# Turning keys and queries by DMA transposes, SBUF to SBUF, in four late steps of a retention and gated-unit kernel

## The chip, the cores and the metric

The kernel runs on one core of one Trainium2 chip. The metric is the device time of one execution in microseconds (us). Ratios and intervals are over fast runs alone; a run is called slow when it lies over 1.5% above the fastest run of the same kernel.

## The reference, cut to what matters

```python
# attention part: 8 batches, 8 heads, 576 positions, head size 64
scores = q @ k.T / 8                       # per batch and head
out    = (scores * Dmat) @ v               # Dmat[i, j] = gamma_h ** (i - j) for i >= j, else 0
x      = out, heads side by side           # 8 x 576 x 512
# gated part
gate   = sigmoid(causal 5-tap convolution of x, per channel)
result = (gate * (x @ w_val)) @ w_out      # 8 x 576 x 512
```

## The kernel before

The sequence is cut into pieces of 256 positions, and a remainder of 64. There are 20 steps, 0 to 19; steps 6, 9, 16 and 19 are the remainders of two batches at once. For each step GpSimd scales and casts keys and queries to bf16 (kb, qb). TensorE turns them in blocks of 128x128 (tpk, tpq, into PSUM), ScalarE copies the keys back and VectorE the queries (kt, qt). TensorE then makes scores (sc) from both, and the share of the carried state (o) from qt.

```python
def transp(s, which="kq"):
    ...
    for nm in which:
        tp = glp.tile([P, HP, R, P], BF16, tag="gps", name="tp" + nm)
        for hp in range(HP):
            for rr in range(R):
                nc.tensor.transpose(tp[:, hp, rr, :], src[:, rr, 2*hp:2*hp+2, :]..., ident)
        t = at.tile([P, HP, R, P], BF16, tag=f"{nm}t{R}", name=nm + "t", bufs=1 + R)
        copy(TE[nm == "q"], t, tp)          # keys: ScalarE, queries: VectorE
        r[nm + "t"] = t
```

The order of work in each step is written out by hand. `T` turns step s+1, `Sa` and `Sb` are the two halves of the scores of step s, `I` its share of the state, `X` the new state of step s+1, and numbers are spaces filled with gated work.

```python
FULL = [["Sa", "T", "4.45", "X", "XS", "0.0", "I", "Sb", "Q3", "G3", "4.9", "Vb", "Va", "E", "B"],
        ["Sa", "4.5", "X", "I", "XS", "Sb", "0.0", "Q3", "G3", "T", "7.15", "Vb", "Va", "E", "B"]]
...
for s in range(NS):
    if s + LOOK < NS:                       # LOOK = 4
        load(s + LOOK)                      # three DMAs from SyncE's queue
    if s > 1 and s + 2 < NS:
        cast(s + 2)                         # GpSimd
    for op in FULL[n] ...:
```

All loads and all output stores are issued by SyncE, one after another.

Of the kernel before, what the change touches and what calls it, by code (L numbers as in the profile page):

```python
# [15 lines left out]
BF16 = mybir.dt.bfloat16  # L16
# [15 lines left out]
def kernel(  # L32
# [10 lines left out]
    nc = tc.nc  # L43
# [3 lines left out]
    P = 128  # L47
# [4 lines left out]
    HP = H // 2  # L52
# [7 lines left out]
    TPS, DSS, CAP = False, False, 2.0  # L60
    PB, EV, TE = [4, 2, 2], "DA", "AD"
    C1, LO = "PPP", "1vo23"
    PATH, TAIL, LASTS = {9: {2: 'D', 3: 'A'}, 11: {2: 'D', 3: 'A'}, 10: {0: 'D', 1: 'A', 2: 'D', 3: 'A'}}, ['w', 'w', 't9.201234', 'w', 'p10.301234', 's10.30', 't10.001234', 's10.31', 'w', 'w', 'w', 'w', 'c9.0', 't10.201234', 'w', 'p11.301', 'w', 'p11.323', 'w', 'p11.34', 's11.30', 'w', 's11.31', 'c11.0', 'v9.0', 'v9.1', 'v9.2', 'v9.3', 't11.201234', 'o9.0', 'o9.1', 'v11.0', 'v11.1', 'v11.2', 'v11.3', 'o11.0', 'o11.1', 'v10.0', 'v10.1', 'v10.2', 'v10.3', 'z10'], [['Sa', '4.5', 'I', 'Sb', 'Q5', 'G5', 'T', '7.15', 'Vb', 'p9.301234', 'Va', 's9.30', 's9.31', 'E', 'B'], ['1.8', 'I', 'Sr', 'p10.101234', '6.65', 'Vr', 's10.10', 'E', 'B', 's10.11']]
    SPL, REMD = 0, [2, 0, 2, 0]
    VC = "P"
# [6 lines left out]
    at = ctx.enter_context(tc.tile_pool(name="at", bufs=3))  # L72
# [19 lines left out]
    NS = len(steps)  # L92
# [130 lines left out]
    def cast(s):  # L223
        u, bb, n = steps[s]
        r = st[s]
        R = 1 if bb is None else 2
        shp = [P, R, H, D]
        f0 = n * 2
        nb = 2 if bb is None else 4
        kb = cs.tile(shp, BF16, tag=f"kb{R}", name="kb", bufs=nb)  # L230
        qb = cs.tile(shp, BF16, tag=f"qb{R}", name="qb", bufs=nb)
        vb = cs.tile(shp, BF16, tag=f"vb{R}", name="vb", bufs=nb)

        how = C1 if s == 1 else "PP" + VC[s % len(VC)]
        for e, dst, src, f in ((how[0], kb, r["kf"], fk), (how[1], qb, r["qf"], fq)):
            (nc.vector if e == "D" else nc.gpsimd).tensor_tensor(  # L236
                dst, src.rearrange("p h r d -> p r h d"),
                f[:, f0:f0 + R, :].unsqueeze(3).to_broadcast(shp), op=ALU.mult)
        vsrc = r["vf"].rearrange("p h r d -> p r h d")
        if how[2] == "A":  # L240
            nc.scalar.copy(vb, vsrc)
        else:
            nc.gpsimd.tensor_copy(vb, vsrc)  # L243
        r.update(qb=qb, kb=kb, vb=vb)

    def transp(s, which="kq"):
        if s >= NS:
            return
        r = st[s]
        R = 1 if steps[s][1] is None else 2  # L250
        for nm in which:
            src = r[nm + "b"]
            tp = (scp if TPS else glp).tile([P, HP, R, P], BF16, tag="sc" if TPS else "gps", name="tp" + nm)
            for hp in range(HP):
                for rr in range(R):
                    nc.tensor.transpose(tp[:, hp, rr, :],  # L256
                                        src[:, rr, 2 * hp:2 * hp + 2, :].rearrange("p a d -> p (a d)"), ident)
            t = at.tile([P, HP, R, P], BF16, tag=f"{nm}t{R}", name=nm + "t", bufs=1 + R)
            copy(TE[nm == "q"], t, tp)
            r[nm + "t"] = t  # L260

    def copy(engine, dst, src):
        if engine == "A":
            nc.scalar.copy(dst, src)  # L264
        else:
            nc.vector.tensor_copy(dst, src)  # L266
# [454 lines left out]
    for s in range(NS):  # L721
# [4 lines left out]
        if s > 1 and s + 2 < NS:  # L726
            cast(s + 2)
        for op in (PART if bb is None else FIRST if s == 0 else SECOND if s == 1 else FULL[n]) if s < NS - len(LASTS) \
# [16 lines left out]
            elif op == "I":  # L745
                inter(s)
            elif op == "T":
                transp(s + 1)
            elif op in ("Tk", "Tq"):
                transp(s + 1, op[1])  # L750
            elif op == "C1":
                cast(1)
            elif op == "C2":
                cast(2)
            elif op[0] == "Q":
                pull(3, int(op[1]))
# [23 lines left out]
            elif op == "B":  # L780
                b = 2 * u + (bb or 0)
# [44 lines left out]
```

## Time and profile before

| | before |
|---|---|
| median, us (all runs of the first comparison) | 182.06 (181.06 to 184.66, 4 runs) |
| span of the profiled run, us | 181.1 |
| TensorE busy | 158.2 us, 87% |
| VectorE / ScalarE / GpSimd busy | 69% / 58% / 60% |
| time of the load and store queue's packets, share of 16 DMA engines | 78.6% |

A busy share is an average over the whole span. What matters here is when: the DMA engines are full for two thirds of the run (8 or 9 tenths in slices 1 to 26 of forty) and mostly free after that (0 to 5 tenths from slice 28 on), TensorE is full nearly to the end (8 or 9 tenths in slices 20 to 38). The prediction below shows those rows, the chain, and the timelines of TensorE and SyncE around step 15.

### The profile page before, as it was taken

Reading aid. Unit: us, or ns where it says so; the run is one execution under the profiler, and the core shown is the slowest. Engines: PE = TensorE matmul, PEld = TensorE weight load, DVE = VectorE, ACT = ScalarE, POOL = GpSimd, SP = SyncE. Lnnn points to the kernel's source line nnn. Section 1 sums busy time; section 2 is a strip of 40 time slices with the busy share of each in tenths; the row PEclk is TensorE's granted clock in tenths of the full one; section 3 lists DMA queues with packets and bytes.
Section 4 is the critical chain, followed back from the end, with each engine's and each line's share of the span. In section 5 each row is a group of like instructions: output and inputs, shape, how many; then the busy total and the mean of one; then the engine's idle time right before and its main releaser. Section 6 shows DMA issues by size and latency. Waiting matters only on the chain.

```text
span 181.1 us, 7638 instructions
## 1 busy us (share of the span) xinstructions
PE 158.2 (87%) x3313; PEld 104.9 (58%) x3313; DVE 125.5 (69%) x240; ACT 105.3 (58%) x216; POOL 109.3 (60%) x105
## 2 busy tenths in 40 slices
PE   0479779967999999979999989998999889999991
PEld 0347557745666666536667567795669534447560
DVE  2968573669669546964669857776859897964931
ACT  6653766545551756237534755653678958689451
POOL 5048299978556958295974974587504697274300
PEclk9999999999999999999999999999999999999999
DMA  5999999999899989999899999997533003205344
GB/s 156 282 295 378 308 260 281 295 289 250 238 309 291 196 217 337 323 267 271 217 364 303 292 183 329 303 296 197 120 118 123 0 0 119 116 4 231 116 100 137
DMA packets 69183, 40.35 MB, mean 223 GB/s; under 512 B 14218, under 2 KB 63646, under 8 KB 69150
## 3 DMA queue, kind: packets, MB, share of 16 engines
q1 hardware_dynamic: 69120, 39.85, 78.6%
q8 instruction: 26, 0.43, 1.0%
q14 instruction: 7, 0.06, 0.1%
q10 hardware_dynamic: 30, 0.01, 0.0%
HBM read 30.42 MB, written 9.44 MB: 220 GB/s over the span
## 4 chain that ended last, share of the span: by engine, by line
PE 68%; DVE 13%; ACT 9%; issue 4%; DMA 3%; SPq 1%; DVEq 0%; ACTq 0%
PE ops L544 17%; PE cps L442 17%; PE vps L537 13%; DVE am L290 5%; PE o L358 4%; PE tpk L256 4%; PE sc L283 4%; ACT gt L448 4%; PE tpq L256 3%; DMA vf<-in_v_dram 3%; DVE accs L468 3%; PE o L345 2%; PE ds L307 2%; ACT kt L264 2%; DVE zt L539 2%
## 5 line engine op out<-in xcount | busy, mean ns | idle before, releaser
L236 POOL TENSOR_TENSOR kb<-kf,fk 128x1024 bf16<-128x1024 f32 (+1 forms) x19 | 32.7, 1723 | 32.9 <-DMA kf<-in_k_dram 32.6
L290 DVE TENSOR_TENSOR am<-sc,mask_c 128x512 bf16<-128x512 f32 x64 | 40.9, 681 | 4.5 <-PE sc L283 4.5
L442 PE MATMUL cps<-xt,diag 64*64 64x512 bf16 (+1 forms) x640 | 35.2, 353 | 1.3 <-ACT xt L264 0.9
L236 POOL TENSOR_TENSOR qb<-qf,fq 128x1024 bf16<-128x1024 f32 (+1 forms) x19 | 32.7, 1723 | 2.9 <-PE tpk L256 1.5
L544 PE MATMUL ops<-wout,zt 128*128 128x512 bf16 x136 | 32.7, 380 | 0.4 <-ACT kt L264 0.3
L442 PEld LDWEIGHTS <-diag 64*64 64x64 bf16 x760 | 25.8, 109 | 11.3 <-issue 3.5
L539 DVE TENSOR_TENSOR zt<-gt,vps 128x256 bf16<-128x256 f32 (+1 forms) x48 | 25.0, 549 | 9.7 <-PE vps L537 5.1
L537 PE MATMUL vps<-xt,wval 128*128 128x512 bf16 (+1 forms) x160 | 31.0, 337 | 0.4 <-DVE qt L266 0.2
L448 ACT ACTIVATE gt<-cps 128x512 f32<-128x512 f32 (+1 forms) x38 | 17.2, 506 | 21.2 <-PE cps L442 21.2
L547 ACT COPY ob<-ops 128x512 f32<-128x512 f32 x34 | 19.7, 585 | 10.0 <-PE ops L544 7.4
L537 PEld LDWEIGHTS <-wval 128*128 128x128 bf16 x192 | 17.7, 97 | 13.2 <-issue 1.9
L264 ACT COPY kt<-tpk 128x1024 bf16<-128x1024 bf16 (+1 forms) x19 | 17.5, 923 | 9.1 <-PE tpk L256 8.9
L243 POOL CAST vb<-vf 128x1024 bf16<-128x1024 f32 (+1 forms) x19 | 18.0, 947 | 4.8 <-DMA vf<-in_v_dram 3.6
L264 ACT CAST xt<-o 128x512 bf16<-128x512 f32 (+1 forms) x17 | 12.2, 720 | 14.2 <-PE o L358 11.6
L544 PEld LDWEIGHTS <-zt 128*128 128x128 bf16 x136 | 12.0, 98 | 14.5 <-DVE zt L539 2.3
L283 PE MATMUL sc<-qt,kt 64*64 64x128 bf16 (+1 forms) x576 | 18.5, 221 | 1.1 <-DVE am L290 0.8
L327 ACT CAST w<-sn 128x256 bf16<-128x256 f32 x30 | 12.0, 406 | 10.3 <-DVE sn L323 7.0
L266 DVE CAST xt<-o 128x512 bf16<-128x512 f32 (+1 forms) x17 | 12.2, 715 | 7.2 <-PE o L358 3.9
L266 DVE COPY qt<-tpq 128x1024 bf16<-128x1024 bf16 (+1 forms) x19 | 11.9, 628 | 6.8 <-PE tpq L256 6.6
L325 DVE TENSOR_TENSOR sn<-ds,sn 128x256 f32<-128x256 f32 x23 | 9.8, 425 | 9.6 <-PE ds L307 6.3
L358 PEld LDWEIGHTS <-vb 64*64 64x64 bf16 x544 | 10.0, 106 | 7.8 <-issue 7.4
L283 PEld LDWEIGHTS <-kt 64*64 64x64 bf16 x576 | 13.2, 109 | 2.1 <-issue 1.9
(90 smaller groups left out, 194.9 us busy)
## 6 DMA issues: line engine op xcount, KB each, us to landing
out_dram<-ob SPq DMA_DIRECT2D x31, 256.0 KB, 3.9
kf<-in_k_dram SPq DMA_DIRECT2D x15, 512.0 KB, 7.2
qf<-in_q_dram SPq DMA_DIRECT2D x15, 512.0 KB, 7.4
vf<-in_v_dram SPq DMA_DIRECT2D x15, 512.0 KB, 7.7
out_dram<-ob SPq DMA_DIRECT2D x10, 128.0 KB, 2.7
wvf<-in_moe_w_val_dram SPq DMA_DIRECT2D x2, 512.0 KB, 7.2
wof<-in_moe_w_out_dram SPq DMA_DIRECT2D x2, 512.0 KB, 8.2
kf<-in_k_dram SPq DMA_DIRECT2D x8, 128.0 KB, 5.0
```

The lines of the kernel that those rows point to most:

```text
L236: (nc.vector if e == "D" else nc.gpsimd).tensor_tensor(dst, src.rearrange("p h r d -> p r h d"), f[:, f0:f0 + R, :].unsqueeze(3).to_broadc ...
L243: nc.gpsimd.tensor_copy(vb, vsrc)
L264: nc.scalar.copy(dst, src)
L266: nc.vector.tensor_copy(dst, src)
L283: nc.tensor.matmul(sc[hh][HS[x], a, rj, :].rearrange("p (r i) -> p r i", r=R), lhsT=r["kt"][HS[hh], hp, rj, HS[x]], rhs=r["qt"][HS[hh], hp ...
L290: nc.vector.tensor_tensor(am, sc[hh], mk.rearrange("p j i x -> p j (i x)").unsqueeze(1).to_broadcast(shp), op=ALU.mult)
L442: nc.tensor.matmul(fold(cps[i][HS[r ^ i]]), lhsT=diag[HS[r], p2, kk, d0 + i, :], rhs=win(d0 + i, kk)[HS[r]], start=(kk == 0 and p2 == 0), ...
L448: nc.scalar.activation(gt, cps[i], AF.Sigmoid)
L537: nc.tensor.matmul(fold(vp), lhsT=wval[:, do, d, :], rhs=win(do, PAD), start=(do == 0), stop=(do == DT - 1))
L539: nc.vector.tensor_tensor(z[0][:, d, 0:N], g[d], vp, op=ALU.mult)
L544: nc.tensor.matmul(op, lhsT=z[0][:, d, m * P:(m + 1) * P], rhs=wout[:, d, :], start=(d == 0), stop=(d == DT - 1))
L547: nc.scalar.copy(ob, op)
```

## The change

The intent is to use the DMA engines' free last third: the keys and queries of steps 15 to 18 are turned by the DMA, straight from SBUF to SBUF, so that TensorE, ScalarE and VectorE are spared the transposes and copies. Step 19 stays as it was.

```diff
+    DTS = [15, 16, 17, 18]
 ...
     def cast(s):
         ...
         r.update(qb=qb, kb=kb, vb=vb)
+        if s in DTS:
+
+            for nm in ("k", "q"):
+                t = at.tile([P, R, HP, P], BF16, tag=f"{nm}t{R}", name=nm + "t", bufs=1 + R)
+                nc.sync.dma_start_transpose(out=t.rearrange("p r a i -> p (r a) i"),
+                                            in_=r[nm + "b"].rearrange("p r h d -> p (r h d)"))
+                r[nm + "t"] = t.rearrange("p r a i -> p a r i")
 
     def transp(s, which="kq"):
-        if s >= NS:
+        if s >= NS or s in DTS:
             return
```

## The prediction

> **What bounds the kernel now.** The first view is the page's table of forty slices (4.5 us each), with the total above it.
>
> ```profile
> PE 158.2 (87%) x3313; PEld 104.9 (58%) x3313; DVE 125.5 (69%) x240; ACT 105.3 (58%) x216; POOL 109.3 (60%) x105
> ...
> PE   0479779967999999979999989998999889999991
> ...
> DMA  5999999999899989999899999997533003205344
> ```
>
> TensorE is the fullest engine, and from slice 20 to the end almost every digit is 8 or 9. The DMA engines are full up to about slice 27 (122 us) and then mostly free. That free third is the reason for the change. The chain that ended last agrees:
>
> ```profile
> PE 68%; DVE 13%; ACT 9%; issue 4%; DMA 3%; SPq 1%; DVEq 0%; ACTq 0%
> PE ops L544 17%; PE cps L442 17%; PE vps L537 13%; DVE am L290 5%; PE o L358 4%; PE tpk L256 4%; PE sc L283 4%; ACT gt L448 4%; PE tpq L256 3%; DMA vf<-in_v_dram 3%; DVE accs L468 3%; PE o L345 2%; PE ds L307 2%; ACT kt L264 2%; DVE zt L539 2%
> ```
>
> The turning of keys and queries (tpk, tpq) is 7% of it over the whole run. Twenty steps are computed, 0 to 19; step 6, 9, 16 and 19 are the half-size remainder steps. I found the four changed steps by counting transposes in TensorE's timeline: steps 15, 16, 17 and 18 are turned at 113.8, 123.7, 128.6 and 132.4 us. The third view is that timeline around step 15 (start, busy us, what):
>
> ```profile
> 113.51 0.39 PE L283 MATMUL sc<-qt,kt 64*64 64x128 bf16 x16
> 113.83 0.62 PE L256 MATMUL tpk<-ident,kb 128*128 128x128 bf16 x8
> 114.29 0.61 PE L256 MATMUL tpq<-ident,qb 128*128 128x128 bf16 x8
> 114.73 1.89 PE L544 MATMUL ops<-wout,zt 128*128 128x512 bf16 x8
> 116.56 0.45 PE L307 MATMUL ds<-vb,kb 64*64 64x64 bf16 x32
> 116.83 0.28 PE L345 MATMUL o<-qt,w 64*64 64x128 bf16 x3
> ```
>
> Step 15 is first used at 116.83 (o<-qt, then the scores), only 3.0 us after its turning begins. [...] whatever comes late here stops everything behind it. The fourth view is the timeline of the queue that issues the DMAs (SyncE):
>
> ```profile
> 109.51 0.63 SPq L106 DMA_DIRECT2D kf<-in_k_dram  x1
> 110.23 1.43 SPq L106 DMA_DIRECT2D qf<-in_q_dram  x1
> 111.75 1.73 SPq L106 DMA_DIRECT2D vf<-in_v_dram  x1
> 113.57 1.46 SPq L106 DMA_DIRECT2D kf<-in_k_dram  x1
> ...
> 118.51 4.39 SPq L575 DMA_DIRECT2D out_dram<-ob  x4
> ```
>
> The loads of step 17 are issued from 109.51 to 113.48, those of step 18 from 113.57. What GpSimd, which casts them, waits for says when they land:
>
> ```profile
> 115.36 1.91 POOL L236 TENSOR_TENSOR kb<-kf,fk 128x1024 bf16<-128x1024 f32 x1 [4.49 <-DMA kf<-in_k_dram]
> 117.22 1.91 POOL L236 TENSOR_TENSOR qb<-qf,fq 128x1024 bf16<-128x1024 f32 x1
> 119.07 1.04 POOL L243 CAST vb<-vf 128x1024 bf16<-128x1024 f32 x1
> ```
>
> The keys issued at 109.51 land at 115.36, 5.9 us later, although one load follows another every 1.6 us: the queue is some four transfers deep. The last of step 17 (vf) has landed by 119.07; I take 118.7.
>
> [...] All loads, stores and the new transposes go through SyncE, so a transpose stands behind the loads issued before it; the 5.9 us above agree. [...] TensorE's pieces here show 219 ns each, but overlap: 8 of them advance the chain by 0.55 (keys) and 0.45 us (queries). No DMA transpose is in this trace. [...] 38 matmuls of cps 64x256 took 2.34 us at 13.84, and 40 of the same took 1.29 us at 159.30.
>
> **The change part by part.**
> *Removed.* 56 transposes on TensorE, three steps of 16 and one of 8. On the chain: 1.0 us for each full step, 0.55 for step 16, 3.55 us in all. Also three kt copies on ScalarE of 1.01 us and one of 0.59, and three qt copies on VectorE of 0.68 us and one of 0.41. These lie almost wholly beside TensorE (of the chain's kt part, the 0.92 us at 111.1 belong to step 14, which keeps it), so I count nothing for them. Best case without new waits: 182.2 - 3.6 = 178.6 us.
> *Unchanged.* The built program's listing shows that on TensorE, VectorE, ScalarE and GpSimd the order is the old one with those instructions taken out. Nothing moves forward into a gap.
> *Added.* Eight DMA transposes on SyncE's queue, 256 KB (128 KB in step 16). Their place in that queue is the point: step 15's pair stands after step 17's loads and before step 18's; step 16's pair after step 18's loads; the pairs of 17 and 18 after four output stores and step 19's loads.
> *Length of one.* Estimate: six remainder loads of 128 KB with rows of 256 B were issued in 100.28 to 107.29 us, 1.17 us each with the queue full; that is 512 rows, 32 per DMA engine, 36 ns a row. The transpose reads 128 x 2048 B in 256-byte pieces (the built program's tile is 16 rows by 128 columns), 64 per engine: 2.3 us, and 1.2 us for a half step. [...]
> *Step 15.* Its casts are done at 106.1, but SyncE reaches the pair only at 113.5, and the queue ahead is empty at 118.7. Keys land at 118.7 + 2.3 = 121.0, queries at 123.3. Without its own turning TensorE is ready at 115.8. It waits 7.5 us; against before step 15 begins 123.3 - 116.8 = +6.5 us late. [...] +1.0 (2.3 against 1.3 us for 40 matmuls, once).
> *Step 16.* 0.55 us saved. Its pair lands near 131, needed (129.6 before, +7) near 136: hidden.
> *Steps 17, 18.* 2.0 us saved. But step 18's loads came 4.6 us later, and the program lets each DMA start only when the eighth one before it has landed; so stores, loads of step 19 and the two pairs are issued one after another from 125 to about 137. Queries of 17 land about 138 (needed 138), of 18 about 143 (needed 141). I add 2.0.
> *Sum.* 6.5 + 1.0 - 0.55 - 2.0 + 2.0 = +7 us, so about 189.2. The chain's part from 136 to 149 is VectorE, busy 13.15 of 14 us in that window; it starts later as a whole and cannot swallow the delay.
>
> **The rivals.**
> *It pays as intended:* transposes hidden, 178.6 us. For: DMA is idle after 130 us, where steps 17 and 18 lie. Against: step 15 would have to land by 116, while the queue in front of it drains at 118.7.
> *Fast transposes, near regular copies[...]:* queries of 15 land about 120.5, +3.7[...], -2.55, no wait in 17 and 18: +1 to +2, 183.5 us, "same".
> *Slow transposes* (5 us or more[...]): step 15 lands near 129, +12; the transfers also hold up step 18's loads, so that 17 and 18 wait several us as well: 197 to 205.
> *Stores held up:* output stores stand behind the transposes of 17 and 18. Four output tiles exist and few are made there; at most 1 us.
>
> **Range and chances.** The middle of my durations gives 189; the transpose's length is the wide term and lies to the long side. Predicted 189.5, range 184 to 203. Faster than 178.6 would be needed for "faster" and only the perfect case gives it: 0.04. Within 2% (to 185.9) needs transposes near 1 us: 0.18. Slower: 0.78.
>
> **What would show it.** Right: one gap on TensorE of 5 to 10 us before step 15's o<-qt, released by the DMA transpose of qt; landing about 8 us after issue (113.5 to 121); matmuls of about 300 ns just after the gap; smaller gaps at 17 or 18; 136 to 149 unchanged in length. Wrong: landing within 4 us of issue (the queue argument falls), gaps mainly at 17 and 18, or a gap of many tens of us (the duration falls).

## The result, and the profile after

| | before | after |
|---|---|---|
| median, us | 182.06 (181.06 to 184.66, 4 runs) | 189.72 (188.12 to 191.77, 4 runs) |
| span of the profiled run, us | 181.1 | 186.4 |
| TensorE busy, us | 158.2 | 157.5 |

The ratio is 1.036, with a 95% interval of 1.028 to 1.045: slower. A ratio here is the mean time of one kernel's fast runs over that of the other's of the same rounds, so not quite the ratio of the medians. Both profiled runs are fast ones. The kernel lost 5 to 8 us, and TensorE's busy time hardly fell although 56 transposes are gone, 3.55 us of the chain: something ran slower.

First the same rows of the page of after (totals; then forty slices, here of 4.66 us; PEclk is TensorE's granted clock in tenths).

```profile
PE 157.5 (84%) x3257; PEld 102.8 (55%) x3257; DVE 123.4 (66%) x236; ACT 101.7 (55%) x212; POOL 109.8 (59%) x105
...
PE   0579879959999998999969999996069898999991
...
PEclk9999999987999999999999999999759999999999
DMA  5999999999999999999999899998893001404444
```

Slices are counted from 0. The 0 on TensorE is slice 28, 130.5 to 135.2 us, and the clock falls to 7 and 5 in slices 28 and 29. (The 8 and 7 at slices 8 and 9 lie long before the changed steps and cost little: the forty cps that began at 46.55 us before begin at 46.70 here.) The DMA engines are full until the end of slice 29 (140 us). The chain that ended last is no longer TensorE's:

```profile
DMA 32%; PE 28%; SPq 10%; DVE 10%; POOL 8%; ACT 6%; issue 4%; DVEq 0%; POOLq 0%
DMA kf<-in_k_dram 19%; PE ops L552 9%; DMA vf<-in_v_dram 7%; PE cps L450 6%; PE vps L545 6%; SPq L104 5%; POOL kb L237 5%; DMA qt<-qb 4%; SPq L107 4%; DVE am L298 3%; DVE accs L476 3%; POOL qb L237 2%; DVE zt L547 2%; PE sc L291 2%; DMA qf<-in_q_dram 2%
```

What lay beside TensorE has become the chain: loads, SyncE's issuing (SPq) and the transposed queries. TensorE's timeline of after shows where it stops (start, busy, engine, line, operation, count; in brackets the idle time before and what ended it):

```profile
118.64 0.42 PE L291 MATMUL sc<-qt,kt 64*64 64x128 bf16 x16 [0.29 <-DMA qt<-qb]
...
129.43 0.32 PE L366 MATMUL o<-am,vb 64*64 64x64 bf16 x16
136.97 0.64 PE L291 MATMUL sc<-qt,kt 64*64 64x128 bf16 x16 [7.22 <-DMA qt<-qb]
137.54 3.07 PE L552 MATMUL ops<-wout,zt 128*128 128x512 bf16 x8
```

The first line is the first use of step 15's turned tiles, the 7.22 us stand before the scores of step 17, and the eight ops after it take 3.07 us where eight of them took 1.89 before: the granted clock was 0.50 from 133.3 to 139.6 us and 1.00 again from 140. "The clock cooled" means no more than this below: a lower granted clock, or, in runs for which it is not given, matmuls that take longer after a stop. The eight ops did not pass the waiting scores here: the last zt that they read was done at 127.2 us, and they began at 137.54. SyncE's timeline of after:

```profile
107.10 0.41 SPq L107 DMA_DIRECT2D kf<-in_k_dram  x1
...
108.56 2.30 SPq L107 DMA_DIRECT2D vf<-in_v_dram  x1
110.95 3.27 SPq L250 DMA_TRANSPOSE kt<-kb  x1
114.34 2.23 SPq L250 DMA_TRANSPOSE qt<-qb  x1
...
124.52 2.79 SPq L583 DMA_DIRECT2D out_dram<-ob  x4
127.36 1.39 SPq L104 DMA_DIRECT2D kf<-in_k_dram  x2
...
132.17 1.28 SPq L250 DMA_TRANSPOSE kt<-kb  x1
133.56 1.27 SPq L250 DMA_TRANSPOSE qt<-qb  x1
```

SyncE issues without a pause from 107 to 138 us. It comes to step 17's queries at 133.56, and the 136.97 on TensorE follows 3.4 us later. The casts it waits for were long done (the queries' at 116.6).

### The profile page after: what moved, and what is told of

Its sections match the earlier page's. It is cut to its first block, busy times and chain, and to the rows that moved or that the text cites.

```text
span 186.4 us, 7535 instructions
## 1 busy us (share of the span) xinstructions
PE 157.5 (84%) x3257; PEld 102.8 (55%) x3257; DVE 123.4 (66%) x236; ACT 101.7 (55%) x212; POOL 109.8 (59%) x105
## 4 chain that ended last, share of the span: by engine, by line
DMA 32%; PE 28%; SPq 10%; DVE 10%; POOL 8%; ACT 6%; issue 4%; DVEq 0%; POOLq 0%
DMA kf<-in_k_dram 19%; PE ops L552 9%; DMA vf<-in_v_dram 7%; PE cps L450 6%; PE vps L545 6%; SPq L104 5%; POOL kb L237 5%; DMA qt<-qb 4%; SPq L107 4%; DVE am L298 3%; DVE accs L476 3%; POOL qb L237 2%; DVE zt L547 2%; PE sc L291 2%; DMA qf<-in_q_dram 2%
## 5 line engine op out<-in xcount | busy, mean ns | idle before, releaser
L552 PE MATMUL ops<-wout,zt 128*128 128x512 bf16 x136 | 33.9, 391 | 0.4 <-ACT kt L272 0.3
L450 PEld LDWEIGHTS <-diag 64*64 64x64 bf16 x760 | 25.3, 109 | 10.5 <-issue 2.4
L272 ACT COPY kt<-tpk 128x1024 bf16<-128x1024 bf16 (+1 forms) x15 | 13.9, 928 | 8.4 <-PE tpk L264 8.3
L274 DVE COPY qt<-tpq 128x1024 bf16<-128x1024 bf16 (+1 forms) x15 | 9.5, 630 | 7.1 <-PE tpq L264 7.0
```

The lines of the kernel that those rows point to most:

```text
L272: nc.scalar.copy(dst, src)
L274: nc.vector.tensor_copy(dst, src)
L450: nc.tensor.matmul(fold(cps[i][HS[r ^ i]]), lhsT=diag[HS[r], p2, kk, d0 + i, :], rhs=win(d0 + i, kk)[HS[r]], start=(kk == 0 and p2 == 0), ...
L552: nc.tensor.matmul(op, lhsT=z[0][:, d, m * P:(m + 1) * P], rhs=wout[:, d, :], start=(d == 0), stop=(d == DT - 1))
```

## The experiments

All outputs were correct. The runs of several kernels spread widely; so I give medians with the range, and the ratio where one was given. Kernels are compared only within the same rounds.

| label | what differs | median, us (range, runs) | before | ratio (95%) | longest waits of TensorE on qt in its profile |
|---|---|---|---|---|---|
| shadow | before, plus the transposes into unread tiles | 181.76 (180.54–184.02, 22) | 181.97 | 0.999 (0.996–1.001) | none |
| swap19 | after, pair 17 ahead of step 19's loads | 185.89 (184.98–187.05, 4) | 181.97 | 1.021 (1.017–1.025) | 3.0 at 15, 2.6 at 18 |
| early | after, pairs 17 and 18 further ahead | 183.16 (180.24–185.77, 22) | 181.97 | 0.998 (0.994–1.002) on 8 fast of 22 | 3.1 at 15 (slow run) |
| d15_16 | only 15 and 16 by DMA | 184.40 (179.86–186.09, 8) | 181.97 | 0.988 on 2 fast of 8 | none (slow run) |
| front | all four pairs as early as casts allow | 184.37 (181.30–186.29, 22) | 181.50 | 1.010 (1.006–1.014) on 8 fast of 22 | 4.7 at 17 (slow run) |
| d18 | only 18 by DMA | 180.98 (179.71–183.80, 18) | 181.50 | 0.998 (0.995–1.000) | none |
| d17_18 | only 17 and 18 by DMA | 183.54 (181.06–185.67, 4) | 181.50 | | 1.4 at 17 (fast run) |
| actq | after, issued by ScalarE | 189.19 (188.76–190.88, 4) | 181.50 | 1.045 (1.040–1.050) | none; waits on ScalarE instead |
| d15 | only 15 by DMA | 186.31 (180.79–187.36, 6) | 181.91 | (1 fast of 6) | 4.5 at 15 (slow run) |
| again | after, unchanged | 190.96 (188.41–191.90, 4) | 181.91 | 1.043 (1.031–1.054) | 3.3 at 15, 5.4 at 17 (slow run) |
| tail | only 17 and 18, 17 ahead of 19's loads | 181.05 (179.77–182.68, 22) | 181.91 | 0.997 (0.994–1.000) | 1.6 at 18 |
| tail2 | only 17 and 18, both ahead of 19's loads | 179.79 (178.55–183.75, 22) | 182.05 | 0.989 (0.987–0.992) | 0.5 at 17 |

Theory A after the first result was: the loss is TensorE waiting for tiles whose transposes stand too far back in SyncE's queue. Rival B: the added DMA work and issue time hurt by themselves. Rival C: a DMA transpose is slow wherever it stands.

### shadow: the same traffic, with nobody waiting for it

```diff
     def transp(s, which="kq"):
-        if s >= NS or s in DTS:
+        if s >= NS:
 ...
         if s in DTS:
             for nm in ("k", "q"):
-                t = at.tile([P, R, HP, P], BF16, tag=f"{nm}t{R}", name=nm + "t", bufs=1 + R)
+                t = at.tile([P, 2, HP, P], BF16, tag=f"{nm}x", name=nm + "x", bufs=1)[:, 0:R]
                 nc.sync.dma_start_transpose(...)
-                r[nm + "t"] = t.rearrange("p r a i -> p a r i")
```

Left out of this diff are the buffer counts that make room for the extra tiles: the half-size kt, qt, kb and qb have one buffer in place of two.

> The kernel before, with all its TensorE transposes and copies, and the same eight DMA transposes issued at the same places of SyncE's queue, into tiles that nobody reads (to make room the half-size kt, qt, kb and qb have one buffer in place of two). Theory A (the loss is TensorE waiting for step 17's qt, which is issued late; the transfers themselves hurt nobody): same as before, 182 to 183 us, no TensorE wait above 1 us. Rival B (the loss is the added DMA work and SyncE time: later loads, later casts, later stores): 185 us or more, with waits on DMA loads or on output buffers.

Measured: ratio 0.999, interval 0.996 to 1.001, on 20 and 39 fast runs. Eight transposes, issued at the places of the change, cost nothing when TensorE does not need them. Rival B falls: later loads, later casts and later stores are swallowed. The loss is the dependence.

### d15_16 and d15: the step where I expected the stop

```diff
-    DTS = [15, 16, 17, 18]
+    DTS = [15, 16]          # d15_16
+    DTS = [15]              # d15
```

> Only steps 15 and 16 turned by DMA; 17 and 18 stay on TensorE. What I predicted (step 15 is where TensorE stops, for some 6 us): 186 to 188 us. Theory A (the profile after shows only 0.3 us of wait at 15 and 0.7 at 16 against 1.55 us saved): 181 to 182.5 us, same as before.

> Only step 15 by DMA. My prediction as written (TensorE stops 7.5 us at step 15 and cools): +6.5 us, 188 us. Reading of the trace after (first use of step 15 is 3.1 us later than I took it, its qt lands within some 3 us of that): between 181 us (landing in time, 1.0 us saved) and 184.5 us (3 us of wait[...]), differing from run to run.

d15_16 gave two runs at 180 and six from 182.8 to 186.1; its ratio of 0.988 rests on the two and I draw nothing from it. d15 gave one run at 180.79 and five from 185.86 to 187.36, while before ran from 180.2 to 183.7. TensorE's timeline of d15, profiled in one of the five:

```profile
123.29 0.64 PE L291 MATMUL sc<-qt,kt 64*64 64x128 bf16 x16 [4.49 <-DMA qt<-qb]
123.69 3.58 PE L450 MATMUL cps<-xt,diag 64*64 64x512 bf16 x40
```

TensorE does stop at step 15, 4.5 us, and the forty cps after it take 3.58 us where they took 2.36 in the profile of before: 1.2 us for the cooled clock (granted: 0.80 in the last 1.3 us of the wait, 0.988 over the run). Less the 1.0 us saved that is +4.7 us, and the five runs lie 4 to 5.5 us above the median of before. The lucky run and the profile of after (0.29 us) show that this wait is not in every execution. The five are slow runs; I take the wait for the kernel's own because the profile names what was waited for, and because swap19, early and again show it too (3.0, 3.1, 3.3 us).

SyncE's timeline of d15 says a part of why:

```profile
112.23 1.58 SPq L107 DMA_DIRECT2D vf<-in_v_dram  x1
113.91 4.38 SPq L250 DMA_TRANSPOSE kt<-kb  x1
118.40 1.31 SPq L250 DMA_TRANSPOSE qt<-qb  x1
```

Directly behind the last of three loads of 512 KB (vf) the transpose of the keys keeps SyncE 4.38 us, against 1.28 us for the same instruction at 132.17 in after. The queries follow at 118.40, and TensorE goes on at 123.29.

The other part is that the DMA engines were not full. These are the 4.5 us of TensorE's wait in d15, by stretches (the stretch and its length; busy time and count of TensorE, its weight loads, VectorE, ScalarE and GpSimd; then granted clock, share of the DMA engines by the sum of packet times, GB/s):

```profile
118.80:119.80 1.00, 0.00 (x0) 0.00 (x0) 0.76 (x1) 1.00 (x2) 1.00 (x1) 1.00 0.14 22
119.80:120.80 1.00, 0.00 (x0) 0.00 (x0) 0.00 (x0) 0.13 (x1) 1.00 (x2) 1.00 2.38 271
120.80:122.00 1.20, 0.00 (x0) 0.00 (x0) 0.00 (x0) 0.00 (x0) 0.66 (x1) 1.00 0.12 6
122.00:123.30 1.30, 0.01 (x3) 0.04 (x4) 0.00 (x0) 0.00 (x0) 0.00 (x0) 0.80 1.16 290
```

For 2.2 of the 4.5 us the DMA engines moved almost nothing (22 and 6 GB/s), although the keys' transpose had been issued by 118.3 and the queries' by 119.7. In the first of these stretches the last packets of vf trickle in (it lands at 120.0); in the second only a few packets of the transposes move. A pause like the second, about 1 us at 5 to 11 GB/s with a transpose waiting, stands also in the profiles of d15_16, d17_18, again, front and tail2. What makes it is open; no run tested it.

One thing stays open. The profile of d15_16 has no wait on qt; TensorE stands still for 1.3 and 2.5 us in the middle of a row of like matmuls, which the profile calls issue, and no semaphore is involved. The trace's packets fit the guess that its instructions arrived late: packets of 16 KB of the instruction queue (q8) end at 113.57 and 125.07 us, and TensorE goes on 1.47 and 1.46 us later; before two shorter stops of this kind in the profile of before (0.81 and 0.50 us) such packets end 1.44 and 1.40 us ahead. Why they came later here no run tested; shadow, with the same transposes in flight, did not slow down.

### again: a second profile of the changed kernel

> The changed kernel once more, for a second profile. If the 7 us wait at step 17 is its mark: again one wait of 6 to 8 us on qt of step 17, at most 3 us at step 15; 188 to 191 us. If waits move from run to run (15 in one, 17 in the other): their sum stays 7 to 9 us.

Measured: 190.96 us. TensorE's timeline of again:

```profile
122.69 0.42 PE L291 MATMUL sc<-qt,kt 64*64 64x128 bf16 x16 [3.29 <-DMA qt<-qb]
122.91 3.46 PE L450 MATMUL cps<-xt,diag 64*64 64x512 bf16 x40
...
140.09 0.64 PE L291 MATMUL sc<-qt,kt 64*64 64x128 bf16 x16 [5.40 <-DMA qt<-qb]
```

Neither form of the expectation holds quite: both steps wait, 8.7 us together, against 7.2 + 0.7 + 0.3 = 8.2 in the first profile (the 0.7 is at step 16). When step 15 waits more, step 17 waits less. The sum of the two profiles differs by 0.5 us; what differs more is how often the clock cools at these waits, once in after (ops of 3.07 us in place of 1.89), twice here (cps of 3.46 in place of 2.36; seven ops in 3.19, where seven took 1.67 in after at 127.82). The profiled runs took 188.1 us (after) and 191.9 us (here); two profiles are too few to say how the other runs divide.

### swap19, early, front: the same four pairs at other places

```diff
-        if s + LOOK < NS:
+        if s + LOOK < NS and s != 15:      # swap19
             load(s + LOOK)
         if s > 1 and s + 2 < NS:
             cast(s + 2)                    # casts, then issues the pair
+        if s == 15:
+            load(s + LOOK)
```

In early, step 17 is cast (and its pair issued) at s == 14 and step 18 at s == 15, before the load of 19. Front does the same and also casts before it loads at s == 13 and 14, so that the pairs of 15 and 16 stand ahead of the loads of 17 and 18.

> The changed kernel with one exchange: step 19's six loads are issued after step 17's two transposes instead of before them. Theory A: the 4.7 us of SyncE time for those loads (127.4 to 132.1) goes from in front of the pair; qt of 17 lands near 131.5 to 132.5, TensorE waits 2 to 3 us in place of 7.2[...]: 183 to 185 us. Rival C (the transposes are slow wherever they stand, the wait is their own length): wait stays above 5 us, 188 us or more.

> The changed kernel with the pair of step 17 issued straight after the pair of 16, ahead of four output stores and step 19's loads, and the pair of 18 ahead of step 19's loads. Theory A: all four pairs land before TensorE needs them, bar under 1 us each at 15 and 16; most of the 3.5 us of removed TensorE work is gained: 178.5 to 180.5 us, 1 to 2% under before. Rival B (added DMA work): 184 us or more. Rival C (slow transposes): wait at 17 still over 3 us, 184 us or more.

> All four pairs by DMA, each issued as early as its casts allow: 15 ahead of step 17's loads, 16 ahead of 18's loads, 17 ahead of the four stores, 18 ahead of 19's loads. Theory A (the loss is only the place in the queue): no TensorE wait on a transpose above 0.5 us anywhere, so nearly all of the 3.5 us is gained: 178.5 to 180.5 us. Rival D (loads of 17 and 18, now later, become the new wait, or the gaps that the profile calls issue grow[...]): 181 to 184 us and no wait on qt.

swap19: the wait at 17 is gone, and about half of the loss with it (fast runs 2.1% over before, where after and again had 3.6% and 4.3%). Rival C falls: the same transposes a few places earlier do not stop TensorE. The time is above what I expected because the waits at 15 (2.95 us) and now at 18 (2.55 us, behind the loads of 19) are still there. early missed its 178.5 to 180.5: the best runs reach 180.2, most lie at 182 to 184, and the profile, from a slow run, has 3.1 us at step 15. Its ratio of 0.998 rests on the 8 runs without the longer times; over all runs its median is 1.2 us above that of before. front missed. TensorE's timeline of front:

```profile
132.68 0.42 PE L291 MATMUL sc<-qt,kt 64*64 64x128 bf16 x16 [4.74 <-DMA qt<-qb]
```

and SyncE's:

```profile
121.33 1.21 SPq L107 DMA_DIRECT2D vf<-in_v_dram  x1
122.64 5.21 SPq L250 DMA_TRANSPOSE kt<-kb  x1
```

The wait at 15 is gone, and step 17 waits instead, 4.7 us: its pair now stands directly behind the loads of 18, which are later because the pairs of 15 and 16 went first, and the first transpose keeps SyncE 5.21 us. None of the three orders is free of waits in its profile. From this I formed theory E: in the part of the run where the DMA engines are full, a pair delays what stands behind it by its own length, and is late itself by the loads ahead of it. Four pairs do not fit before step 17 is needed; one or two late ones do. The last clause is what tail and tail2 test; the rest stays a theory, and the stretches of d15 above, in which the engines stand nearly idle, speak against "full" and "by its own length".

### actq: another queue

```diff
-                nc.sync.dma_start_transpose(
+                nc.scalar.dma_start_transpose(
```

> The changed kernel with all eight transposes issued by ScalarE, in its own queue, in place of SyncE. Theory A (SyncE's order is the cause): the pairs no longer stand behind loads and stores; waits on qt under 1.5 us each, but ScalarE spends some 1.3 us of issue on each of eight: 180 to 184 us. Rival C (slow transposes): wait at 17 remains above 5 us, 188 us.

Measured: 189.19 us, ratio 1.045; my 180 to 184 missed, although no wait on qt is left. The list of TensorE's waits in actq (what waited, for what: us in total, times, longest) shows the largest new one:

```profile
PE ds L315 <- ACT gt L456: 6.2, 3, 4.1
```

ScalarE issued each transpose in 1.2 to 3.4 us, 16.1 us for the eight, in order with its own work: the first two transposes were issued from 105.70 to 110.80, and the gate activations that free PSUM began at 110.84, so they came late. In shadow the issue time on SyncE cost nothing (ratio 0.999); here, on an engine that TensorE waits for, 6.2 of the 16.1 us stand again as TensorE's waits on the gates, and the kernel takes 189.2 us where before takes 181.5.

### d18, d17_18, tail, tail2: only the late steps

```diff
-    DTS = [15, 16, 17, 18]
+    DTS = [18]                 # d18
+    DTS = [17, 18]             # d17_18, tail (with the edit of swap19), tail2
 ...
-        if s + LOOK < NS:
+        if s + LOOK < NS and s != 15:                  # tail2
             load(s + LOOK)
-        if s > 1 and s + 2 < NS:
+        if 1 < s and s + 2 < NS and s != 16:
             cast(s + 2)
+        if s == 15:
+            cast(18)
+            load(s + LOOK)
```

> Only step 18 by DMA, at the place the change gave it. Theory A: issued near 128, lands near 132, first used near 137.5, so hidden; 1.0 us saved: 181 us, same as before. If removing 16 transposes gains nothing even when hidden (TensorE not the bound there): 182 us and longer VectorE waits.

> Steps 17 and 18 by DMA, 15 and 16 on TensorE. Theory A: without the two earlier pairs SyncE reaches step 17's pair some 4 us sooner, near 128, qt lands near 132.5, first use 131: wait about 1.5 us, not cold, against 2.0 us saved: 181.5 to 182.5 us. If the place behind step 19's loads alone makes the loss: wait of 4 us or more and cooling, 185 us or more.

> Only steps 17 and 18 by DMA, and the pair of 17 issued ahead of step 19's loads (18's behind them). Theory E (a pair is free when no large load stands before it in the queue and it is issued 6 us ahead of its use; adding pairs 15 and 16 uses DMA time that the loads of 17 and 18 need): no wait on qt, 2.0 us saved: 179.5 to 180.7 us, 0.6 to 1.2% under before. If pairs late in the run cost something of their own: 181.5 us or more, with a wait on qt or longer VectorE waits.

> Only steps 17 and 18 by DMA, both pairs issued back to back ahead of step 19's loads (casts of 18 brought forward by a step for it). Theory E: the 1.6 us of wait on qt of 18 that the kernel with 18's pair behind those loads showed goes away, no wait on a transpose is left, and 1 to 2 us come off before: 179.7 to 180.9 us. If step 18's pair was not the cause of that wait, or the end is set elsewhere: 181 us, as that kernel.

d18 came out as expected, though its gain of 0.4 us (difference of the means of fast runs) is within the noise. d17_18 has four runs: two lie at 181.1 and 182.1, two at 184.9 and 185.7, so the expected 181.5 to 182.5 is not confirmed. Its profile, the run at 181.06, has the 1.4 us at step 17 that was expected, and its granted clock is 0.998 over the run, so "not cold" held; the two long runs have no profile. tail is 0.3% under before and still waits 1.6 us for the queries of 18, which stand behind the loads of 19; the pair of 17, whose issue begins at 122.71, 7.6 us before its use at 130.35, is not waited for. (The 6 us of the expectation were my estimate; no run looked for the limit.) tail2 moves that pair ahead of them too, and is 1.1% faster than before, with an interval of 0.8 to 1.3%; 1.1% of 182 us is about the 2.0 us that turning two full steps costs on TensorE. SyncE's timeline of tail2:

```profile
123.45 2.15 SPq L250 DMA_TRANSPOSE kt<-kb  x1
125.70 1.27 SPq L250 DMA_TRANSPOSE qt<-qb  x1
127.07 1.27 SPq L250 DMA_TRANSPOSE kt<-kb  x1
128.45 1.95 SPq L250 DMA_TRANSPOSE qt<-qb  x1
130.45 1.39 SPq L104 DMA_DIRECT2D kf<-in_k_dram  x2
```

The only wait on a transpose left in its profile (a run of 181.23 us, one of its longer ones) is 0.5 us at step 17. This version beats both kernels.

## Why the prediction was right or wrong

The time was 189.7 us for a predicted 189.5, and "slower" had 0.78. The mechanism was right: TensorE stands still for a transpose that comes late out of SyncE's queue (7.2 us in after, 4.5 in d15), and what follows in its order stands with it (the eight ops of after). That the number was met within 0.3 us is partly luck: the wait at 15 and the length of a transpose were put too high, the wait at 17 was left out, and these errors cancelled. By the prediction's own list the first profile is mixed: the gap is "mainly at 17 and 18" (7.2 of 8.2 us), which stood under "Wrong"; the keys of step 15 landed 6.3 us after issue there and 8.4 in d15, not within 4, so the queue argument was not refuted.

- **Nothing without a wait, best case -3.55 us.** Right for steps 17 and 18: tail2 gains about the 2.0 us that were counted for them.
- **Length of one transpose, 2.3 us.** Too long. It was an estimate from the issue times of six loads of 128 KB, with no transpose in the trace; that the range of 184 to 203 reached so far to the long side was my estimate too. In d17_18, from 130.0 to 131.6 us, when nothing but transposes moved:

```profile
DMA packets 1853, 0.46 MB, mean 286 GB/s; under 512 B 1853, under 2 KB 1853, under 8 KB 1853
```

  That is 0.9 us for 256 KB, close to the speed of the loads (301 GB/s in the profile of before from 113 to 124 us). Where SyncE issued four in a row every 1.38 us (after, 133.7 to 138.4 us) they moved at 207 GB/s, 1.3 us each. The sum of packet times cannot serve as a measure here: it is 128% of the engines' time in that window of d17_18, and over the profiles its surplus per full transpose lies anywhere from 1.5 to 3.6 us. The time from the start of issue to landing is longer, 3.1 us for the last queries of d17_18's row of four, and the time that SyncE is held is another thing again: at least 1.25 us for 256 KB (tail) and 1.20 us for 128 KB (early), and 2.5 to 5.2 us for the first of a pair directly behind three loads of 512 KB (2.47 for the half step in early, 5.21 in front).
- **"Keys land at 118.7 + 2.3 = 121.0, queries at 123.3".** The last number was met, by errors that cancel: in d15, whose order is the same up to there, the loads ahead had landed at 120.0 and not 118.7, the keys landed at 122.3, and TensorE goes on at 123.29, 1.0 us after them. In again and early, which also come to the pair at 113.5, it goes on at 122.69 and 123.17. In the first profile of after it was 118.64, because that run had come to the pair some 3 us earlier.
- **"Step 15 is first used at 116.83".** This is the step that failed. The o<-qt and scores at 116.83 are the second half of step 14: the table of the order has `I` and `Sb` of step 14 after `T`. Step 15's own scores are later; in TensorE's timeline of before twelve of the sixteen are this line:

```profile
119.94 0.36 PE L283 MATMUL sc<-qt,kt 64*64 64x128 bf16 x12
```

  So TensorE had 3.1 us more, and the wait at step 15, predicted as 7.5 us, was 4.5 in d15, 3.3 in again and 0.3 in the first profile of after.
- **Steps 17 and 18, "I add 2.0".** Too small by 3 to 5 us, and at the wrong step: they were meant for step 18, which waited for no transpose in after or again, and step 17 was to wait for nothing. "Queries of 17 land about 138" was right (TensorE went on at 136.97 and, in again, at 140.09). "Needed 138" was not: it held only with the full delay of step 15 in front. Without it the scores of 17 were ready to go at 129.75, and the wait was 7.2 us (5.4 in again). So the misreading at step 15 reached step 17 too, with the opposite sign.
- **Why the sum held.** The end is set by when step 17's queries land, and that is a matter of SyncE's order. A delay at 15 only eats into the wait at 17. The prediction did not argue this. From the first profile of after: 0.3 + 0.7 + 7.2 us of waits, 1.2 for the cooled clock, less 3.55, is +5.8; the spans differ by 5.3. From again: 8.7 of waits, 1.9 for each of two cooled stretches (122.69 to 127.76 took 5.1 us, where the same work took 3.2 in after; 140.09 to 144.19 took 4.1, where it took 2.2 in swap19), less 3.55, is +8.9 against +9.1 of span.
- **Clock, +1.0 once.** Before the result nothing had shown that a wait cools the clock: the prediction had slow matmuls at the start of the run alone (sc took 309 ns on average from 13 to 16.2 us and 219 from 20 to 60), with a granted clock of 1.00 there. So it was my estimate, and it held. It cost 1.1 to 1.2 us in the group of matmuls right after the gap (again at step 15, d15, after), more with the work behind that group, and it came twice in the profile of again. How long a wait has to be no run settles. Forty cps, 2.36 us before, took 3.48 and 3.81 us after waits of 2.55 and 2.95 us (swap19, steps 18 and 15), 3.46 after 3.29 (again) and 4.51 after 3.11 (early), but 2.36 after 1.63 us (tail). The length alone does not decide: after a stop of 2.52 us (d15_16) eight vps took their usual 1.90 us.
- **Step 16 hidden.** Nearly: 0.7 us of wait in the first profile.
- **"136 to 149 unchanged in length".** Right. From the cps at 135.85 to the ops at 149.49 us it was 13.64 us before, and from 141.26 to 154.90 after, 13.64 us: it follows the delay as a whole and swallows none of it.
- **The rivals.** Slow transposes (5 us or more) fell with the 0.9 to 1.3 us. Fast transposes (at the 301 GB/s of the loads before, 256 KB take 0.9 us, and two of them after 118.7 give the 120.5) came nearer to the length than the prediction's own 2.3, but their +1 to +2 us did not come: they assumed no wait at 17. "It pays as intended" fell for four steps; tail2 has it for two. Stores held up cost nothing, as shadow shows (0.999).

## What to carry to other kernels

The DMA engines' free last third was of use here only to work that could be queued there (four steps: 1.036 times the time of before; two late steps, well placed: 0.989): look for the place in the issuing queue, count what stands ahead of it and when the result is first read, and move the transfer past large loads that are not urgent (with both pairs ahead of step 19's loads the longest wait was 0.5 us in tail2, with one behind them 1.6 in tail). Find the first reader by the program's own order, not by the nearest instruction with the right name. Keep DMA issuing off engines that the bottleneck waits for (actq: 16.1 us of issue on ScalarE, 189.2 us against 181.5).
